# Quarter-array state products in a retention layer, and other issue times for a routed expert stage

## The chip, the cores and the metric

The kernel runs on one core of a Trainium2 chip. The metric is the device time of one execution in microseconds, the median of the runs. Five engines work side by side, each with its own instruction queue: TensorE (PE, matrix products; PEld is its loading of weights), VectorE (DVE), ScalarE (ACT), GpSimd (POOL) and SyncE (SP, which here only issues DMAs). They meet through semaphores.

## The reference

Three layers follow each other, all in fp32.

1. A retention layer: 8 sequences, 8 heads, 576 positions, head size 64. The scores are `q @ k.T / 8`, multiplied elementwise by `gamma_h ** (i - j)` for `j <= i` (0 elsewhere), and then multiplied by `v`. There is no softmax.
2. A first expert layer on the 4608 rows of 512: each row goes to the expert (of 8) with the largest cosine logit, `out = gate * (relu(x @ w1[e]) @ w2[e])` with 1024 hidden columns.
3. A second expert layer of 8 experts with a capacity of 576 rows each: all 4608 x 8 logits are sorted in falling order, and each is granted if its row is still free and its expert not yet full; then `relu(x @ w1[e]) @ w2[e]`.

```python
for idx in order:
    tok, e = (int(idx) // E, int(idx) % E)
    if assigned[tok] >= 0 or counts[e] >= cap:
        continue
    assigned[tok] = e
    counts[e] += 1
```

## The kernel before, in words

**Attention (lines 312 to 629).** The 4608 rows are 36 tiles of 128 rows; `T` counts them, `i = T % 9` is the place within a pair of sequences (nine tiles hold two sequences of 576 rows; in tile `i == 4` one sequence ends and the next begins). The eight heads are kept as four pairs `hp`, and a pair's two heads `e = 0, 1` stand in the two halves of the 128 partitions. The retention matrix is computed chunk by chunk: within a tile the scores `k.T q` are formed (`s_qk`, L401), weighted with the decay table (L404) and multiplied by `v` (`s_pv`, L419); what earlier tiles of the sequence contribute comes through a state per head of 64 x 64, which `s_state` accumulates in PSUM (L437) and copies to SBUF (L443). The state product is L415. Before the change the copy of the state is a block-diagonal 128 x 128 matrix per head pair (`bd`, two buffers whose other blocks are set to zero once), so that one product handles both heads with the whole array. The result `o` of a tile takes one PSUM bank, and ACT copies it out as `xT` (L422).

`s_out` (one tile later) computes routing logits from `xT` (L457, on four groups of 32 columns of the array) and transposes it back to rows (L463, into the PSUM tile `tp`, two buffers), which ACT copies out (L464). `s_sel` (two tiles later) finishes the logits (L472). Groups of up to five tiles are then routed (`route`): ranks by a product, destination rows by DVE, and scatters of the rows to DRAM on POOL's queue (L533). The order in which one loop step issues these parts is written out by hand at lines 592 to 622: loads of tile `T + 3` on SP's queue, `s_qk(T+1)`, `s_sel(T-2)`, `s_pv(T)`, a piece of routing, `s_state(T)`, `s_kd(T+2)`, `s_out(T-1)`. From tile 31 on the first expert weights are loaded and split into a high and a low part (`w_conv`: ACT L266, POOL L271).

A product of fp32 operands is two instructions in the trace, each with its own weight load, so 8 products are 16 instructions.

**First expert layer (lines 1221 to 1345).** Experts one after the other, three products per tile pair (high x high, high x low, low x high), rows loaded from the scattered copy in DRAM.

**Second expert layer (lines 1369 to 1536).** For each expert `p`: `search(p)` finds by bisection which logits are granted to it, in seven rounds, each of which goes through PE three times (counts L875, a fold L888, a decision L950) and through DVE between them; `members(p)` turns the chosen rows into an index list (L1106), POOL gathers the rows (five indirect DMAs, L1380), PE transposes them (L1400) and ACT and DVE split them (L1408, L1410); then come the first layer (`ffn1`, L1456) and the second (`ffn2`, L1495, and L1489 and L1491 for the last, half tile). Searches of later experts run beside the layers of earlier ones.

Their order on each engine is set by a planner, the class `Issue`: it keeps a clock for PE, DVE, ACT and POOL, and lets threads (the searches, member lists, splits, evacuations) issue their next step when its time by these clocks has come; PE's own layer products move PE's clock on. Its numbers are guesses at durations, and they decide only the order of issue. Two of them matter here:

- the sixth field of a thread, `early`: a thread's step on PE that follows a step on another engine is due `HOP["P"] - early` = 0.25 - early after it. A negative value makes the planner leave more time before it puts that step into PE's order. `search` and `members` get 0.7 for expert 0, 0.0 for expert 1 and `LAZY` = -0.35 for the others.
- `XGAT[p][t]`: when the planner thinks that gathered tile `t` has landed, its issue on POOL plus 3.2. `xtr2` lets the transposes into PE's order from then on (and from when the tile two before it has been split).

Of the kernel before, what the change touches and what calls it, by code (L numbers as in the profile page):

```python
# [9 lines left out]
F32 = mybir.dt.float32  # L10
# [3 lines left out]
AF = mybir.ActivationFunctionType  # L14
# [5 lines left out]
B, H, S, D = 8, 8, 576, 64  # L20
N, DM, E, FF = 4608, 512, 8, 1024
NT = N // 128
# [18 lines left out]

def constants():
    g = 1.0 - 2.0 ** (-5.0 - np.arange(H, dtype=np.float64))
    p = np.arange(128)
# [4 lines left out]
    for e in range(2):  # L49
        for hp in range(4):  # L50
            gq[64 * e:64 * e + 64, hp, :] = (g[2 * hp + e] ** s / 8.0)[None]
            gs[64 * e:64 * e + 64, hp, :] = (g[2 * hp + e] ** np.array([128.0, 256.0, 384.0]))[None]
# [11 lines left out]
    for nj in (32, 4, 2):  # L64
# [11 lines left out]
        "c_dt": np.ascontiguousarray(dt.reshape(128, 4, 2, 128).transpose(0, 2, 1, 3)).astype(f), "c_gq": gq.astype(f), "c_gs": gs.astype(f),  # L76
# [81 lines left out]
def moe_kernel(ctx: ExitStack, tc: tile.TileContext, moe_expert_emb, moe_tau, moe_w1, moe_w2,  # L158
# [153 lines left out]
    with tc.tile_pool(name="actab", bufs=1) as tab, \  # L312
# [20 lines left out]
        bd = []  # L333
        for i in range(2):
            t = tab.tile([128, 4, 128], F32, name=f"bd{i}")
            (G if i else V).memset(t, 0.0)
            bd.append(t)
# [69 lines left out]
        def s_pv(T):  # L407
            i = T % 9
            nq = nq_of(i)
            vt, sm = TL[T]["vr"], SM.pop(T)  # L410
            op_ = ps.tile([128, 4, 128], F32, name="o")
            if nq:
                qs, bdl = QS.pop(T), BD.pop(T)
                for hp in range(4):
                    P.matmul(op_[:, hp, :nq], bdl[:, hp, :], qs[:, hp, :nq], start=(hp == 0), stop=False,  # L415
                             skip_group_check=True)
            for hp in range(4):
                for e in range(2):
                    P.matmul(op_[64 * e:64 * e + 64, hp, :], vt[:, 2 * hp + e, :], sm[:, e, hp, :],  # L419
                             start=(hp == 0 and not nq), stop=True, skip_group_check=True)  # L420
            xT = wk.tile([128, 4, 128], F32, name="xT")
            A.activation(xT, op_, AF.Copy)  # L422
            XTT[T] = xT

        def s_state(T):
            i = T % 9
            t = TL.pop(T)
            if i == 8:
                return
            vt = t["vr"]  # L430
            r0 = 64 if i == 4 else 0
            kd = KDT.pop(T)
            if i in (0, 4):
                st_ps[0] = ps.tile([128, 4, 128], F32, name="st")
            for hp in range(4):
                for e in range(2):
                    P.matmul(st_ps[0][64 * e:64 * e + 64, hp, 64 * e:64 * e + 64], kd[r0:, 2 * hp + e, :],  # L437
                             vt[r0:, 2 * hp + e, :], start=(i in (0, 4) and hp == 0), stop=(i in (3, 7)),
                             skip_group_check=True)
            nb = bd[i % 2]  # L440
            for e in range(2):
                z = slice(64 * e, 64 * e + 64)
                A.activation(nb[z, :, z], st_ps[0][z, :, z], AF.Copy)  # L443
            BD[T + 1] = nb

        def s_out(T):
# [14 lines left out]
            xp = ps.tile([128, 4, 128], F32, name="tp", bufs=2)  # L461
# [409 lines left out]
    def search(p):  # L871
# [152 lines left out]
        IS.spawn(members(p, rk), p if p < 2 else 3, IS.t["V"], (0.7, 0.0, LAZY)[min(p, 2)])  # L1024
# [18 lines left out]
    NQ, LAZY = 4, -0.35  # L1043
# [17 lines left out]
    def members(p, rk):  # L1061
# [48 lines left out]
        XGAT[p] = [IS.t["G"] - 1.25 * (T2 - 1 - t) + 3.2 for t in range(T2)]  # L1110
# [4 lines left out]
    def chain():  # L1115
        for p in range(E):
            yield lambda: 0.0
            CHT[0][1] = (0, 3, 2)[min(p, 2)]
            CHT[0][5] = (0.7, 0.0, LAZY)[min(p, 2)]
            yield from search(p)  # L1120
# [454 lines left out]
```

## Time and profile before

| | |
|---|---|
| median of three timed runs | 1272.17 us (1271.94 to 1278.58) |
| profiled execution: its own time | 1273.87 us |
| profiled execution: span, mean granted clock | 1272.1 us, 0.969 |
| PE busy, share of the span | 1197.8 us, 94% |
| DVE, ACT, POOL busy | 716.4, 578.7, 326.3 us |
| attention, first to last score-value product | about 13 to 195 us |
| second expert layer, from its first product | about 746 to 1265 us |

The shares are averages over stages with different limits, so a stage is read from its own windows and its own order of time. PE's busy time is modelled from overlapping instructions; in its order of time the distances from one group's start to the next group's start are what work costs. The granted clock is 1.00 at 2.4 GHz and 0.50 at 1.2 GHz.

### The profile page before, as it was taken

The page shows a single profiled execution, that of the slowest core. Times are in us where ns is not written, and L with a number is a line of the kernel's source. Part 1 is how long each engine was busy: PE and PEld are TensorE (multiplying, and loading weights), DVE is VectorE, ACT ScalarE, POOL GpSimd, SP SyncE. Part 2 cuts the span into 40 slices and gives each one's busy share as a digit, 9 for nine tenths or more (in the row PEclk, how much of TensorE's full clock was granted, in tenths as well). Part 3 has the DMA queues.
Part 4 walks back from the last instruction along what each step waited for, and adds up shares of the span by engine and source line. Part 5 has one row for each costly group of instructions (what it writes and reads, how often), then busy time and mean ns, then how long its engine had stood idle before and what let it go on. Part 6 is the DMA issues. An engine that isn't in the chain of part 4 may idle for free. (4 is left out here: it accounts for less than half of the span.)

```text
span 1272.1 us, 23381 instructions
## 1 busy us (share of the span) xinstructions
PE 1197.8 (94%) x8855; PEld 1026.9 (81%) x8855; DVE 716.4 (56%) x2332; ACT 578.7 (45%) x1090; POOL 326.3 (26%) x451
## 2 busy tenths in 40 slices
PE   6999985899999999999999969998989899999997
PEld 5888874889898989899887667785968688788896
DVE  4466643767566757566666755656565657562120
ACT  3566653345454545453632152534434444455450
POOL 3253454613030313030100020404131313243211
PEclk9999986999999999999999979998989999999999
DMA  8898863576776868685851252938484737578841
GB/s 270 271 284 281 274 229 125 211 175 180 191 196 171 209 163 217 155 231 137 229 130 35 99 152 65 257 75 245 98 230 81 222 98 193 139 188 217 211 92 38
DMA packets 91741, 224.63 MB, mean 177 GB/s; under 512 B 13671, under 2 KB 14447, under 8 KB 91488
## 3 DMA queue, kind: packets, MB, share of 16 engines
q0 software_dynamic: 28272, 90.35, 32.6%
q1 hardware_dynamic: 63344, 132.67, 31.3%
q8 instruction: 72, 1.18, 0.4%
q14 instruction: 53, 0.43, 0.1%
HBM read 130.26 MB, written 40.28 MB: 134 GB/s over the span
## 5 line engine op out<-in xcount | busy, mean ns | idle before, releaser
L1167 DVE SCALAR_TENSOR_TENSOR jk<-yr,wgb 128x512 bf16<-128x512 f32 x168 | 115.4, 687 | 2.4
L1246 ACT ACTIVATE hh<-l 128x320 fp32r<-128x320 f32 x128 | 55.4, 433 | 120.1 <-PE l L1245 106.2
L1438 DVE SCALAR_TENSOR_TENSOR h2l<-l,h2h 128x288 fp32r<-128x288 f32 (+2 forms) x128 | 58.3, 457 | 79.0 <-ACT h2h L1436 78.6
L1247 DVE SCALAR_TENSOR_TENSOR hl<-l,hh 128x320 fp32r<-128x320 f32 x128 | 62.4, 487 | 66.4 <-ACT hh L1246 60.9
L251 POOL DMA_DIRECT2D w_0l<-raw x29 | 26.2, 903 | 285.8 <-ACT w_0l L248 247.2
L1333 ACT ACTIVATE yr<-l,gts 128x512 f32<-128x512 f32 x40 | 27.5, 688 | 152.1 <-PE l L1321 70.8
L1436 ACT ACTIVATE h2h<-l 128x288 fp32r<-128x288 f32 (+2 forms) x128 | 52.3, 409 | 90.5 <-PE l L1456 89.8
L1470 POOL DMA_INDIRECT out_dram<-o,tid x40 | 41.0, 1025 | 162.8 <-ACT o L1463 122.4
L404 DVE TENSOR_TENSOR sm<-s,dt 128x512 f32<-128x512 f32 (+1 forms) x80 | 48.0, 633 | 55.3 <-PE s L401 43.8
L1463 ACT ACTIVATE o<-l 128x512 f32<-128x512 f32 (+1 forms) x40 | 23.8, 595 | 111.2 <-PE l L1495 79.5
L1380 POOL DMA_INDIRECT xg<-ybuf,idx x40 | 43.0, 1075 | 75.4 <-SPq L1348 53.4
L717 DVE TENSOR_TENSOR xl<-tp,xh 128x512 fp32r<-128x512 f32 (+1 forms) x41 | 27.6, 676 | 53.1 <-ACT xh L716 53.1
L401 PE MATMUL s<-qT,kT 64*128 64x128 f32 x576 | 45.0, 297 | 11.2 <-DMA qT<-qT 9.1
L931 DVE TENSOR_TENSOR cmp<-v,kb 128x1280 bf16<-128x1280 f32 (+1 forms) x42 | 54.4, 1295 | 0.2
L401 PEld LDWEIGHTS s<-qT,kT 64*128 64x128 f32 x576 | 37.7, 198 | 17.4 <-DVE nw_u L168 4.9
L1243 PE MATMUL l<-xh,w_0h 128*128 128x320 f32 x128 | 40.9, 319 | 10.3 <-DVE hl L1247 5.7
L378 POOL TENSOR_TENSOR kd<-kr,gk 128x512 f32<-128x512 f32 (+1 forms) x32 | 34.5, 1080 | 59.8 <-PE st L437 23.9
L251 POOL DMA_DIRECT2D w_3l<-raw x29 | 24.8, 854 | 94.1 <-ACT w_3l L248 70.6
L533 POOL DMA_INDIRECT xs<-xg,r_sli x36 | 36.9, 1024 | 46.8 <-ACT xg L464 26.3
L1408 ACT ACTIVATE xh<-tp 128x512 fp32r<-128x512 f32 (+1 forms) x40 | 22.0, 552 | 58.6 <-PE tp L1400 44.2
L422 ACT ACTIVATE xT<-o 128x512 f32<-128x512 f32 x36 | 21.5, 597 | 59.0 <-PE o L419 51.6
L251 POOL DMA_DIRECT2D w_2l<-raw x29 | 25.2, 868 | 88.9 <-ACT w_2l L248 64.1
(374 smaller groups left out, 4084.0 us busy)
## 6 DMA issues: line engine op xcount, KB each, us to landing
raw<-in_moe_w_dram SPq DMA_DIRECT2D x128, 512.0 KB
w_0l<-raw POOLq DMA_DIRECT2D x29, 512.0 KB
w_1l<-raw POOLq DMA_DIRECT2D x29, 512.0 KB
w_2l<-raw POOLq DMA_DIRECT2D x29, 512.0 KB
w_3l<-raw POOLq DMA_DIRECT2D x29, 512.0 KB
ybuf<-yr SPq DMA_DIRECT2D x40, 257.0 KB
xt<-xs SPq DMA_DIRECT2D x39, 261.0 KB
kT<-kT SPq DMA_DIRECT2D x36, 256.0 KB
```

The costliest lines, as they stand in the source:

```text
L251: G.dma_start(lo, RAW[wpos[1]], accum_op=OP.add)
L401: P.matmul(sp[e][:, hp, :], kT[r, hp, :], qT[r, hp, :], start=True, stop=True, skip_group_check=True)
L404: V.tensor_tensor(sm[z, e, :, z], sp[e][z, :, z], dt_t[z, e, :, z], op=OP.mult)
L931: V.tensor_tensor(cmp, bc(v, ALLC, nj), kb.bitcast(F32)[:, None, :].to_broadcast([128, NSL, nj]), op=OP.is_ge)
L1167: V.scalar_tensor_tensor(jk, yr[:, :DM], 1.0, wgb[:, j, :], op0=OP.mult, op1=OP.mult, accum_out=L2V[:, cc, j:j + 1])
L1243: P.matmul(pp, wh[:, fz], xh[:, kk, z], start=(kk == 0), stop=False)
L1246: A.activation(hh[:, f, z], pp, AF.Relu)
L1247: V.scalar_tensor_tensor(hl[:, f, z], pp, 0.0, hh.bitcast(F32)[:, f, z], op0=OP.max, op1=OP.subtract)
L1380: G.indirect_dma_start(out=xg[:m, t, :], out_offset=None, in_=ybuf, in_offset=bass.IndirectOffsetOnAxis(ap=idx[:m, t:t + 1], axis=0))
L1436: A.activation(h2h[:, f, z], pq, AF.Relu)
L1438: V.scalar_tensor_tensor(h2l[:, f, z], pq, 0.0, h2h.bitcast(F32)[:, f, z], op0=OP.max, op1=OP.subtract)
L1470: st = G.indirect_dma_start(out=out, out_offset=bass.IndirectOffsetOnAxis(ap=TID[p][:m, t:t + 1], axis=0), in_=o[:m], in_offset=None)
```

## The change

It has three parts.

1. The state is kept dense, 128 x 64 per head pair, with one copy per tile instead of two. Each state product becomes two products, each on a quarter of the array (64 rows by 64 columns). So that four products that follow each other name the four quarters, the two heads of every odd pair change places in the partitions (`head`), in the tables and in the laid-out inputs `kT` and `qT`; the results go back to the places they had. Pairs of even and odd number write to two PSUM banks, so `o` takes two banks, and the transposes' tile `tp` has one buffer instead of two. The score-value product L419 names the array's column halves in the order low, high, high, low.
2. In the second expert layer the planner's landing time of gathered rows is 4.8 instead of 3.2 for all experts but the first.
3. `LAZY` has a value for each expert.

```diff
--- before.py
+++ after.py
@@ -39,6 +39,10 @@
 LOG2E = 1.4426950408889634
 
 
+def head(e, hp):
+    return 2 * hp + (e ^ (hp & 1))
+
+
 def constants():
     g = 1.0 - 2.0 ** (-5.0 - np.arange(H, dtype=np.float64))
     p = np.arange(128)
@@ -48,8 +52,8 @@
     gq, gs = np.empty((128, 4, 128)), np.empty((128, 4, 3))
     for e in range(2):
         for hp in range(4):
-            gq[64 * e:64 * e + 64, hp, :] = (g[2 * hp + e] ** s / 8.0)[None]
-            gs[64 * e:64 * e + 64, hp, :] = (g[2 * hp + e] ** np.array([128.0, 256.0, 384.0]))[None]
+            gq[64 * e:64 * e + 64, hp, :] = (g[head(e, hp)] ** s / 8.0)[None]
+            gs[64 * e:64 * e + 64, hp, :] = (g[head(e, hp)] ** np.array([128.0, 256.0, 384.0]))[None]
     tl = np.arange(9)[None, :, None]
     pos = 128 * tl + p[:, None, None]
     pos = np.where(pos >= S, pos - S, pos)
@@ -73,7 +77,7 @@
     s16[np.arange(16), np.arange(16) % E] = 1.0
     return {
         **blk, "c_s16": s16,
-        "c_dt": np.ascontiguousarray(dt.reshape(128, 4, 2, 128).transpose(0, 2, 1, 3)).astype(f), "c_gq": gq.astype(f), "c_gs": gs.astype(f),
+        "c_dt": np.stack([np.stack([dt[:, head(e, hp)] for hp in range(4)], 1) for e in range(2)], 1).astype(f), "c_gq": gq.astype(f), "c_gs": gs.astype(f),
         "c_gk": gk.reshape(128, 72).astype(f), "c_sel": sel.astype(f),
         "c_id": np.eye(128, dtype=f), "c_tri": tri.astype(f),
     }
@@ -330,11 +334,7 @@
         dt_t = tab.tile([128, 2, 4, 128], F32, name="dt")
         SY.dma_start(dt_t, c["c_dt"])
         load_tile(0, ("vr", "kr"))
-        bd = []
-        for i in range(2):
-            t = tab.tile([128, 4, 128], F32, name=f"bd{i}")
-            (G if i else V).memset(t, 0.0)
-            bd.append(t)
+        bd = [tab.tile([128, 4, 64], F32, name=f"bd{i}") for i in range(2)]
         taub = tab.tile([128, 1], F32, name="taub")
         SY.dma_start(taub, ap(moe_tau, 0, [[0, 128], [1, 1]]))
         emb = tab.tile([E, DM], F32, name="emb")
@@ -408,18 +408,25 @@
             i = T % 9
             nq = nq_of(i)
             vt, sm = TL[T]["vr"], SM.pop(T)
-            op_ = ps.tile([128, 4, 128], F32, name="o")
+            op_ = ps.tile([128, 2, 512], F32, name="o")
+
+            def o(e, hp, n):
+                c0 = 64 * (e ^ (hp & 1))
+                return op_[c0:c0 + 64, hp & 1, 128 * (hp >> 1):128 * (hp >> 1) + n]
             if nq:
                 qs, bdl = QS.pop(T), BD.pop(T)
                 for hp in range(4):
-                    P.matmul(op_[:, hp, :nq], bdl[:, hp, :], qs[:, hp, :nq], start=(hp == 0), stop=False,
-                             skip_group_check=True)
+                    for e in range(2):
+                        r = slice(64 * e, 64 * e + 64)
+                        P.matmul(o(e, hp, nq), bdl[r, hp, :], qs[r, hp, :nq], start=(hp < 2), stop=False,
+                                 skip_group_check=True)
             for hp in range(4):
                 for e in range(2):
-                    P.matmul(op_[64 * e:64 * e + 64, hp, :], vt[:, 2 * hp + e, :], sm[:, e, hp, :],
-                             start=(hp == 0 and not nq), stop=True, skip_group_check=True)
+                    P.matmul(o(e, hp, 128), vt[:, head(e, hp), :], sm[:, e, hp, :],
+                             start=(hp < 2 and not nq), stop=True, skip_group_check=True)
             xT = wk.tile([128, 4, 128], F32, name="xT")
-            A.activation(xT, op_, AF.Copy)
+            A.activation(xT.rearrange("p (j s) n -> p s j n", s=2),
+                         op_[:, :, :256].rearrange("p s (j n) -> p s j n", j=2), AF.Copy)
             XTT[T] = xT
 
         def s_state(T):
@@ -431,16 +438,14 @@
             r0 = 64 if i == 4 else 0
             kd = KDT.pop(T)
             if i in (0, 4):
-                st_ps[0] = ps.tile([128, 4, 128], F32, name="st")
+                st_ps[0] = ps.tile([128, 4, 128], F32, name="st")[:, :, :64]
             for hp in range(4):
                 for e in range(2):
-                    P.matmul(st_ps[0][64 * e:64 * e + 64, hp, 64 * e:64 * e + 64], kd[r0:, 2 * hp + e, :],
-                             vt[r0:, 2 * hp + e, :], start=(i in (0, 4) and hp == 0), stop=(i in (3, 7)),
+                    P.matmul(st_ps[0][64 * e:64 * e + 64, hp, :], kd[r0:, head(e, hp), :],
+                             vt[r0:, head(e, hp), :], start=(i in (0, 4) and hp == 0), stop=(i in (3, 7)),
                              skip_group_check=True)
             nb = bd[i % 2]
-            for e in range(2):
-                z = slice(64 * e, 64 * e + 64)
-                A.activation(nb[z, :, z], st_ps[0][z, :, z], AF.Copy)
+            A.activation(nb, st_ps[0], AF.Copy)
             BD[T + 1] = nb
 
         def s_out(T):
@@ -458,7 +463,7 @@
                          skip_group_check=True)
             part = wk.tile([128, 128], F32, name="part")
             A.activation(part, lp[:, :128], AF.Copy)
-            xp = ps.tile([128, 4, 128], F32, name="tp", bufs=2)
+            xp = ps.tile([128, 4, 128], F32, name="tp")
             for hp in range(4):
                 P.transpose(xp[:, hp, :], xT[:, hp, :], ident)
             A.activation(xg[:, i, :DM], xp.rearrange("p a n -> p (a n)"), AF.Copy)
@@ -1021,7 +1026,7 @@
             V.scalar_tensor_tensor(sn[:, z], sn[:, z], r2[:, z:z + 1], mem[:, z], op0=OP.add, op1=OP.mult)
         V.scalar_tensor_tensor(rk, sn[:, 0], 1000.0, sn[:, 1], op0=OP.add, op1=OP.add)
         LST.append(p)
-        IS.spawn(members(p, rk), p if p < 2 else 3, IS.t["V"], (0.7, 0.0, LAZY)[min(p, 2)])
+        IS.spawn(members(p, rk), p if p < 2 else 3, IS.t["V"], LAZY[p])
         if p < E - 1:
             yield "V", 1.2
             fo = tl("fo", (128, E))
@@ -1040,7 +1045,7 @@
 
     LST, MDONE, CHT = [], {}, []
     shf = sw.tile([128, 256], BF, name="shf")
-    NQ, LAZY = 4, -0.35
+    NQ, LAZY = 4, (0.7, 0.0, 0.0, -0.2, -0.35, -0.5, -0.5, -0.5)
 
     RROK = {}
 
@@ -1107,7 +1112,7 @@
         MDONE[p] = IS.t["V"]
         yield lambda: GATHER[0](p)
         yield "G", 1.25 * T2
-        XGAT[p] = [IS.t["G"] - 1.25 * (T2 - 1 - t) + 3.2 for t in range(T2)]
+        XGAT[p] = [IS.t["G"] - 1.25 * (T2 - 1 - t) + (4.8 if p else 3.2) for t in range(T2)]
         XG2[p] = GATHER[1](idx)
 
     GATHER = [lambda p: None, None]
@@ -1116,7 +1121,7 @@
         for p in range(E):
             yield lambda: 0.0
             CHT[0][1] = (0, 3, 2)[min(p, 2)]
-            CHT[0][5] = (0.7, 0.0, LAZY)[min(p, 2)]
+            CHT[0][5] = LAZY[p]
             yield from search(p)
 
     with tc.tile_pool(name="mb", bufs=1, reuse_waits="tile") as mb, tc.tile_pool(name="mw", bufs=2, reuse_waits="tile") as mw, \
@@ -1559,7 +1564,8 @@
     q, k, v = (np.asarray(inputs[n]) for n in ("q", "k", "v"))
     laid = {nm: np.ascontiguousarray(a.transpose(0, 2, 1, 3)).reshape(N, DM) for nm, a in (("kr", k), ("vr", v))}
     for nm, a in (("kT", k), ("qT", q)):
-        t = a.transpose(1, 3, 0, 2).reshape(4, 2, D, NT, 128)
+        t = a.transpose(1, 3, 0, 2).reshape(4, 2, D, NT, 128).copy()
+        t[1::2] = t[1::2, ::-1].copy()
         laid[nm] = np.ascontiguousarray(t.transpose(3, 1, 2, 0, 4)).reshape(NT, 128, 4, 128)
     laid["w_gate_t"] = np.ascontiguousarray(np.asarray(inputs["moe2_w_gate"]).T)
     for name, a in laid.items():
```

## Rows read from the trace of the kernel before

**Rows 1.** Windows by stage: engines' busy time, granted clock, DMA share, GB/s.
```profile
20.00:160.00 140.00, 139.22 (x1983) 118.32 (x1982) 84.72 (x215) 85.24 (x225) 53.39 (x74) 0.99 0.85 280
160.00:212.00 52.00, 34.94 (x405) 28.56 (x404) 21.57 (x91) 24.37 (x59) 26.34 (x34) 0.81 0.47 167
...
735.00:1272.00 537.00, 507.19 (x3394) 422.27 (x3394) 263.01 (x813) 236.13 (x448) 139.18 (x180) 0.95 0.60 153
```

**Rows 2.** PE's timeline, one tile of attention: start, us, line, tiles, instructions.
```profile
114.42 0.42 PE L457 MATMUL lg<-xT,enT 128*32 128x128 f32 x8
114.78 0.66 PE L463 MATMUL tp<-ident,xT 128*128 128x128 f32 x4
...
116.46 0.39 PE L472 MATMUL lg<-sel,part 128*128 128x8 f32 x2
116.70 1.14 PE L415 MATMUL o<-qs,bd 128*128 128x128 f32 x8
117.77 1.09 PE L419 MATMUL o<-sm,vr 128*64 128x128 f32 x16
118.69 0.64 PE L437 MATMUL st<-vr,kd 128*64 128x64 f32 x16
119.26 0.43 PE L457 MATMUL lg<-xT,enT 128*32 128x128 f32 x8
```

**Rows 3.** The same view, a tile that has no state product.
```profile
102.64 0.39 PE L472 MATMUL lg<-sel,part 128*128 128x8 f32 x2
102.96 1.09 PE L419 MATMUL o<-sm,vr 128*64 128x128 f32 x16
```

**Rows 4.** All instructions of the state product's line on PE.
```profile
L415 PE MATMUL o<-qs,bd x256: 275/275/580, 20.1 to 193.2; 128*128 128x128 f32 x112, 128*128 128x64 f32 x16
```

**Rows 5.** Windows of 20 us in attention, the one with the highest DMA share.
```profile
60.00:80.00 20.00, 19.50 (x284) 16.76 (x285) 14.41 (x34) 12.28 (x35) 10.86 (x15) 1.00 0.94 296
```

**Rows 6.** ACT's timeline, the copy of the transposed tile.
```profile
116.25 0.59 ACT L464 ACTIVATE xg<-tp 128x512 f32<-128x512 f32 x1
```

**Rows 7.** Timelines of POOL, ACT and PE around tile 32; in brackets the idling before.
```profile
165.07 1.04 POOL L378 TENSOR_TENSOR kd<-kr,gk 64x512 f32<-64x512 f32 x1 [5.03 <-DMA xs<-xg,r_sli]
...
176.63 1.06 ACT L266 ACTIVATE w_0h<-raw 128x1024 fp32r<-128x1024 f32 x1 [6.53 <-DMA raw<-in_moe_w_dram]
...
179.34 0.59 PE L472 MATMUL lg<-sel,part 128*128 128x8 f32 x2 [4.65 <-ACT part L460]
```

**Rows 8.** Line L875, counts of searches 1 and 2 (ten instructions each).
```profile
L875 PE MATMUL srb<-oh,cmp x60: 176/176/190, 752.6 to 781.1; 128*128 128x32 bf16 x50, 128*16 128x32 bf16 x10
...
L875 PE MATMUL srb<-oh,cmp x70: 176/176/190, 804.4 to 846.0; 128*128 128x32 bf16 x60, 128*16 128x32 bf16 x10
```

**Rows 9.** PE's timeline at the turns from one expert to the next.
```profile
815.69 0.46 PE L1400 MATMUL tp<-ident,xg 64*128 64x64 f32 x4
...
880.01 0.66 PE L1400 MATMUL tp<-ident,xg 128*128 128x128 f32 x4 [1.56 <-DMA xg<-ybuf,idx]
...
890.04 0.61 PE L1456 MATMUL l<-xh,w_0h 128*128 128x288 f32 x1
...
945.01 0.63 PE L1400 MATMUL tp<-ident,xg 128*128 128x128 f32 x4 [1.72 <-DMA xg<-ybuf,idx]
946.93 1.09 PE L1400 MATMUL tp<-ident,xg 128*128 128x128 f32 x4 [1.29 <-DMA xg<-ybuf,idx]
...
1016.99 0.66 PE L1400 MATMUL tp<-ident,xg 128*128 128x128 f32 x4 [2.16 <-DMA xg<-ybuf,idx]
```

**Rows 10.** POOL's timeline, the second gather of expert 3.
```profile
938.71 1.01 POOL L1380 DMA_INDIRECT xg<-ybuf,idx  x1 [0.30 <-issue]
```

**Rows 11.** Windows with the clock at its lower level, columns as in rows 1.
```profile
881.80:895.40 13.60, 11.74 (x55) 9.09 (x56) 8.39 (x20) 4.36 (x11) 0.91 (x1) 0.50 0.28 85
946.60:953.50 6.90, 6.57 (x19) 4.69 (x20) 3.25 (x7) 1.18 (x3) 1.06 (x2) 0.51 0.47 164
1018.30:1021.70 3.40, 3.40 (x20) 2.71 (x19) 1.19 (x4) 0.52 (x2) 0.00 (x0) 0.50 0.54 187
```

## The prediction

> **What bounds the kernel now.** I read the windows by stage first, then TensorE's own order of time in both stages that the diff touches, then what its late instructions waited for. Each row of [rows 1] gives a stretch, its length, the busy time and instruction count of PE, PEld, DVE, ACT and POOL, the granted clock, the DMA share and GB/s. From 20 to 160 us, tiles of attention, PE is busy 139.22 of 140 us: whatever shortens PE's work there shortens the stage. From 160 to 212 us it is busy 34.94 of 52: there a chain through weights and scatters rules. From 735 us on, the second expert stage, PE is busy 507.19 of 537 at a granted clock of 0.95: what can be won without removing PE work is some 30 us of idling and what the 0.50 level costs.
>
> **Part 1, dense states.** A tile's period is 119.26 - 114.42 = 4.84 us [rows 2]. Between the start of the selection product (L472) and the start of the score-value product (L419) lie 1.31 us, which hold the four state products of L415, each two instructions: 8 on the whole array. The change makes them 16 on quarters of it.
>
> No row has quarter products, so I bound them. In tiles without a state L419 starts 0.32 us after L472 [rows 3]: that is what the change of array shape costs, and the change now pays it ahead of its own first product, then the change of shape into L419, as before. The nearest row with four at once is L457: its 8 instructions on four column groups take 0.36 us to the next group, two rounds of four, draining included. L419's 16, in eight rounds of two, take 118.69 - 117.77 = 0.92, so 0.115 a round. With four at once, L415 needs four rounds: 0.36 + 2 x 0.115 = 0.59, and L472 to L419 becomes 0.32 + 0.59 = 0.91: **0.40 us less a tile**. With two at once it is eight rounds: 0.36 + 6 x 0.115 + 0.32 = 1.37, 0.06 more than now. One after the other it is sixteen: 2.29, 0.98 more. I take four at once: the halves overlap by columns in L419, and by columns four at a time in L457, and consecutive products of the change name four different quarters.
>
> There are 256 / 8 = 32 such tiles [rows 4]; the four of 64 columns I count like the others. Not all of it arrives. At tile 32 PE waits 4.65 us at 179.34 for an activation that stands behind the first weight conversion, which starts at 176.63 when its weights land; SP issues them behind a load that waits for scatters, and POOL at 165.07 waits for those same scatters' landing [rows 7]. That chain is released about tile 29 and then runs at its own pace, so what tiles 29 to 31 save only lengthens the wait: 29 tiles count, 29 x 0.40 = 11.6, less 0.6 for the first tiles, where PE waits for loads: **-11 us**.
>
> What hides the rest. The copy of the state, one 128x256 activation for two of 64x256, leaves ACT less to do; ACT is 85 of 140 us busy [rows 1], so nothing, and at most some tenths at the tail. The copy xT reads two banks, the same 512 columns: between 0 and 0.1 us a tile, hidden for the same reason. The transposes' PSUM tile is now single: the copy out of it starts at 116.25 and takes 0.59 [rows 6], and the next transposes come at about 119.6, 2.4 us of cover even at the shorter period; without that cover each tile would lose what is missing of 0.59. L419 now alternates its column halves as low, high, high, low. Pairs remain, so zero; if the places where one half follows itself (three a tile) cost a round each, 3 x 0.115 x 36 = 12 us. I take zero, since pairs are what L419 needs. The removed memsets stand beside the first loads: nothing.
>
> Loads must keep up. A tile moves about 1.3 MB; the densest stretch, 60 to 80 us, shows 296 GB/s at a share of 0.94 [rows 5], and 280 GB/s on the mean of 20 to 160. At 4.44 us a tile the mean becomes 280 x 4.84 / 4.44 = 305. Free capacity is nearly gone, but loads run three tiles ahead; zero, with 4 us as the other end.
>
> **Part 2, the second stage's order.** Here nothing is added or removed; the planner's numbers decide where in PE's order the search's products and the transposes of gathered rows stand. For search 2 the slack before each PE step goes from 0.35 to 0, for search 3 from 0.35 to 0.2, for searches 5 to 7 from 0.35 to 0.5. Search 1 already has 0: its six counts run from 752.6 to 781.1, 5.7 us a round; search 2's seven from 804.4 to 846.0, 6.9 a round [rows 8]. With three PE steps a round, 3 x 0.35 = 1.05 is the planned difference. Seven rounds and four further steps make 8.8; I take **8 us earlier for the index list of expert 2**.
>
> What that buys stands at the turn from expert 1 to 2: the transposes at 880.01 wait 1.56 us for gathered rows, little of the second layer is left to run by then, and expert 2's first layer starts at 890.04 [rows 9]. From 881.8 to 895.4 the clock is 0.50 (the 1.2 GHz level, after the idling) and PE is busy 11.74 of 13.6 us [rows 11]: lost are 1.56 + 1.9 idle and half of 11.74, 9.3 us together. Eight us earlier, second-layer products still cover most of the landing. What stays is the landing itself: the second gather of expert 3 ends its issue at 938.71 + 1.01, and its transposes run at 946.93, 7.2 us later [rows 9, 10]; the planner allowed 3.2, now 4.8, so some 2 us of waiting plus a short fall of the clock stay: gain 2 to 9.3, I take 6.
>
> At the turns 2 to 3 and 3 to 4 there is product work left, so 1.6 us more allowance turns 1.6 us of waiting (1.72 + 1.29 at 945 to 947; 2.16 at 1017) into products [rows 9], and may save the falls of the clock, worth half of 6.57 and of 3.40 busy us [rows 11]. Gains 1.6 to 4.9 and 1.6 to 3.3; I take 2.5 and 2. At the turn 0 to 1 the last transposes at 815.69 stand just before the end of the second layer's products and no wait is seen [rows 9]: pushed back by 1.6 they are exposed, with their split behind them. Cost 0 to 4, I take 2. Queued behind them is all of expert 1's first layer. Later turns show no such wait; searches 5 to 7 get slower by 7 x 3 x 0.15 = 3 us each, against an 8 us head start: zero. Sum: -6 - 2.5 - 2 + 2 = **-8.5 us**.
>
> **Total.** The profiled execution took 1273.87 us, its span 1272.1 and 1.8 around it; the three timed runs' median, 1272.17, lies 1.7 below. 1273.87 - 11 - 8.5 = 1254.4 on that execution, 1252.7 on the median: **1253**.
>
> **Rivals.**
> 1. *Two quarters at a time* (0.12). The first two products of each four use different row halves and write one PSUM bank. L401, the one product here with two row halves, writes two banks, so no row shows such a pair running together. If bank sharing forbids it, rounds hold two, L472 to L419 takes 1.37, and attention gains nothing (2 us lost): 1272.2 + 2 - 8.5 = 1265.7. The Trainium skill, TensorEngine Tiling (Array Packing), Restrictions and Gotchas, says that different row tiles cannot access the same PSUM bank simultaneously; by that rule this rival is the outcome, and no run shown so far tests it.
> 2. *The reordering gives nothing* (0.14). The landing is 7.2 us, not 4.8, so every turn still waits and the clock still falls, and the turn 0 to 1 pays 4: only attention's 11 remain: 1261. For it: the allowance is still 2.4 short. Against it: 8 us of search time are read from two searches side by side.
> 3. *Loads bind* (0.07). At 305 GB/s the queue falls behind and 4 to 6 us of attention's gain go to waits of L401 for qT or kT: 1258.
> 4. *Slower* (0.05). Quarter products run one at a time. Place: L415, 32 tiles; price 0.98 each, 31 us, none of it absorbed; it decides from more than eight rounds a tile on. 1272.2 + 31 - 8.5 = 1295. Against it: L419's halves overlap.
>
> The forecast itself has 0.62, its own range 1245 to 1261. The range to hold the time 8 in 10 reaches to rivals 2 and 3 and most of 1: 1243 to 1265. What a measurement of this kernel tells from no change is about 0.5%, 6.4 us: faster than 1265.8 takes 0.61 of the forecast and 0.24 of rivals 1 to 3, 0.85; within it 0.09 (halves of rivals 1 and 2); slower 0.06.
>
> **What would show it.** Right: L415 as 512 instructions of 64*64; L419 starting 0.9 us after L472; a period near 4.44; the wait at tile 32 a microsecond longer; search 2's rounds under 6 us; no long 0.50 stretch at the turn 1 to 2, and transposes of expert 3 waiting 1.4 us or less. Wrong: 1.3 us or more between L472 and L419, waits of L401 for loads in mid-stage, or transposes that wait as long as before although they stand later; a longer pause at the turn 0 to 1 than 4 us would eat the second part.

## The result and the profile after

The changed kernel takes 1253.04 us (median of four runs, 1251.50 to 1253.45) against 1273.45 for the kernel before beside it; the ratio is 0.983, 95% interval 0.980 to 0.986. Run once more on another chip (below) it took 1247.84 against 1274.44, ratio 0.980, interval 0.977 to 0.982. The forecast was 1253. That the number fits so well is partly luck, as the stages show: two terms were off and a third, unforeseen one made up for it.

The profiled execution took 1252.89 us, its span is 1251.1, which is 21.0 less than before. Cut at the first product of each expert layer, the span up to its last product divides like this (us; 7.2 us follow the last product in both kernels):

| | before | after | forecast | measured |
|---|---|---|---|---|
| attention, to the first product of expert layer 1 | 212.3 | 202.4 | -11 | -9.9 |
| expert layer 1, to the first product of the second | 534.1 | 538.8 | 0 | +4.7 |
| second stage: expert 0 (turn 0 to 1 in it) | 70.2 | 72.0 | +2 | +1.8 |
| experts 1, 2, 3 together | 217.2 | 199.0 | -10.5 | -18.2 |
| experts 4 to 7 together | 231.1 | 231.7 | 0 | +0.6 |

**Attention.** The windows of the changed kernel, with the columns of [rows 1]; the line numbers are larger by five to seven than before from L415 on.

```profile
20.00:160.00 140.00, 136.41 (x2299) 112.05 (x2301) 85.68 (x228) 80.67 (x209) 54.64 (x77) 0.99 0.87 291
...
725.00:1251.00 526.00, 498.69 (x3404) 418.65 (x3404) 266.54 (x818) 237.95 (x451) 140.84 (x180) 0.97 0.62 157
60.00:80.00 20.00, 19.95 (x345) 16.41 (x347) 15.65 (x41) 12.02 (x32) 9.21 (x15) 1.00 0.92 295
```

PE is nearly as full as before from 20 to 160 us (136.41 of 140 us, where it was 139.22), in 316 more instructions. The loads still keep up: 291 GB/s on the mean. PE's order of time in one tile, which answers to [rows 2], and the list of all instructions of the state product, which answers to [rows 4]:

```profile
107.58 0.42 PE L462 MATMUL lg<-xT,enT 128*32 128x128 f32 x8
...
109.62 0.39 PE L477 MATMUL lg<-sel,part 128*128 128x8 f32 x2
109.93 0.67 PE L421 MATMUL o<-qs,bd 64*64 64x128 f32 x16
110.53 1.09 PE L425 MATMUL o<-sm,vr 128*64 128x128 f32 x16
111.46 0.64 PE L444 MATMUL st<-vr,kd 128*64 128x64 f32 x16
112.02 0.43 PE L462 MATMUL lg<-xT,enT 128*32 128x128 f32 x8
```
```profile
L421 PE MATMUL o<-qs,bd x512: 218/269/356, 19.0 to 182.4; 64*64 64x128 f32 x149, 64*64 64x64 f32 x22
```

The tile's period is 112.02 - 107.58 = 4.44 us, where it was 4.84. L477 to L425 is 110.53 - 109.62 = 0.91 us, where it was 1.31. The next line starts 0.60 us after the 16 instructions of the quarter products began (0.59 forecast). That they are four rounds of four can be read from the single instructions in the trace: they start in groups of four, each group within 0.02 us, at 109.93, 110.09, 110.20 and 110.31. L425 to L444 is 0.93, as before, so the order low, high, high, low of its column halves costs nothing. The end of the stage, in brackets the idling before (answers to [rows 7]): first the line of the kernel before that takes `kd`, without a wait; then PE and POOL of the changed kernel.

```profile
166.38 0.68 PE L437 MATMUL st<-vr,kd 64*64 64x64 f32 x16
```
```profile
159.05 0.83 PE L444 MATMUL st<-vr,kd 64*64 64x64 f32 x16 [2.18 <-POOL kd L378]
166.35 0.42 PE L462 MATMUL lg<-xT,enT 128*32 128x128 f32 x8 [0.52 <-DVE slot L525]
171.12 0.39 PE L477 MATMUL lg<-sel,part 128*128 128x8 f32 x2 [2.66 <-ACT part L465]
175.48 1.16 PE L401 MATMUL s<-qT,kT 64*128 64x128 f32 x16 [0.95 <-DMA qT<-qT]
181.27 0.66 PE L468 MATMUL tp<-ident,xT 128*128 128x128 f32 x4 [0.92 <-ACT xg L469]
```
```profile
157.84 1.17 POOL L378 TENSOR_TENSOR kd<-kr,gk 64x512 f32<-64x512 f32 x1 [6.55 <-DMA xs<-xg,r_sli]
```

The POOL instruction that stands behind the scatters is released at 157.84 instead of 165.07, 7.2 us earlier, while PE is ready for its result at 159.05 - 2.18 = 156.87 instead of 166.38, 9.5 earlier. So PE now waits for `kd` where it had not to before, and the wait for the first weights has shrunk from 4.65 to 2.66. The last row is the single `tp` buffer: it costs 0.92 us once.

**Second stage.** The transposes of gathered rows at the turns 1 to 2, 2 to 3 and 3 to 4, and the first layer of expert 2 (answers to [rows 9]); none has a wait in brackets any more (before there were six such waits, 8.3 us together; [rows 9] has four of them, and the other two are shown here first):

```profile
881.79 1.09 PE L1400 MATMUL tp<-ident,xg 128*128 128x128 f32 x4 [1.13 <-DMA xg<-ybuf,idx]
...
1018.09 0.94 PE L1400 MATMUL tp<-ident,xg 128*128 128x128 f32 x4 [0.45 <-DMA xg<-ybuf,idx]
```

```profile
870.19 1.04 PE L1405 MATMUL tp<-ident,xg 128*128 128x128 f32 x8
...
882.57 0.30 PE L1461 MATMUL l<-xh,w_0h 128*128 128x288 f32 x1
...
928.42 1.03 PE L1405 MATMUL tp<-ident,xg 128*128 128x128 f32 x8
...
991.58 1.03 PE L1405 MATMUL tp<-ident,xg 128*128 128x128 f32 x8
```

And the windows over these turns (columns as above): the clock is 1.00 throughout, where [rows 11] had 23.9 us at 0.50. The first line is a new stretch at 0.50, which stands behind the turn 0 to 1, after two waits of PE for search steps (1.12 and 0.40 us).

```profile
814.80:818.20 3.40, 3.40 (x16) 3.40 (x15) 1.92 (x3) 1.57 (x3) 0.00 (x0) 0.50 0.49 166
868.00:950.00 82.00, 80.53 (x576) 64.32 (x575) 50.73 (x159) 35.09 (x70) 22.50 (x32) 1.00 0.61 161
950.00:1020.00 70.00, 69.69 (x506) 57.76 (x505) 40.55 (x134) 34.70 (x65) 21.57 (x25) 1.00 0.64 160
```

All of the gain in experts 1 to 3 is waiting and clock: in their 217.2 us before, PE stood idle for 13.0 and lost 10.9 to the lower clock (half of its busy time at 0.50), in the 199.0 after it is 3.7 and 1.7. What remains is 193.4 and 193.5.

**Where the transfers stand.** SP and POOL up to expert 3's gather, first of the kernel before, then of the changed one. The SP row covers several weight loads of 512 KB (x3, x2); `xg` is a gather, `w_2l` and `w_3l` are the 512 KB transfers that finish a weight block.

```profile
933.46 10.05 SPq L239 DMA_DIRECT2D raw<-in_moe_w_dram  x3
932.36 0.85 POOL L251 DMA_DIRECT2D w_2l<-raw  x1 [3.68 <-PE srb L950]
...
934.88 0.87 POOL L251 DMA_DIRECT2D w_3l<-raw  x1 [0.33 <-issue]
937.35 1.06 POOL L1380 DMA_INDIRECT xg<-ybuf,idx  x1 [1.60 <-DVE idx L1106]
```
```profile
920.09 3.47 SPq L243 DMA_DIRECT2D raw<-in_moe_w_dram  x2
920.90 1.07 POOL L1385 DMA_INDIRECT xg<-ybuf,idx  x1 [2.54 <-PE srb L955]
922.28 1.42 POOL L1385 DMA_INDIRECT xg<-ybuf,idx  x1 [0.30 <-issue]
...
927.42 1.01 POOL L255 DMA_DIRECT2D w_2l<-raw  x1
...
929.77 0.92 POOL L255 DMA_DIRECT2D w_3l<-raw  x1
```

Before, the gather of expert 3 came behind the transfers of `w_2l` and `w_3l` and amid three loads; now it comes ahead of `w_2l` and `w_3l`, with two loads beside it. Measured from the start of the expert whose products run, it is earlier by 937.35 - 890.04 - (920.90 - 882.57) = 9.0 us.

### The profile page after: what moved, and what is told of

The parts are those of the page before. It is cut to its first block, busy times and chain, and to the rows that moved or that the text cites. A ratio compares the mean times of both kernels' runs of the same rounds, so it can differ in the third digit from the quotient of the medians.

```text
span 1251.1 us, 23851 instructions
## 1 busy us (share of the span) xinstructions
PE 1181.0 (94%) x9111; PEld 1012.0 (81%) x9111; DVE 715.4 (57%) x2331; ACT 567.6 (45%) x1058; POOL 326.5 (26%) x450
## 5 line engine op out<-in xcount | busy, mean ns | idle before, releaser
L401 PE MATMUL s<-qT,kT 64*128 64x128 f32 x576 | 44.8, 296 | 11.5 <-DMA qT<-qT 9.7
L401 PEld LDWEIGHTS s<-qT,kT 64*128 64x128 f32 x576 | 37.6, 198 | 17.9 <-issue 5.7
L255 POOL DMA_DIRECT2D w_1l<-raw x29 | 25.1, 867 | 88.9 <-ACT w_1l L252 61.8
```

What stands on the lines that cost most here:

```text
L255: G.dma_start(lo, RAW[wpos[1]], accum_op=OP.add)
L401: P.matmul(sp[e][:, hp, :], kT[r, hp, :], qT[r, hp, :], start=True, stop=True, skip_group_check=True)
```

## The experiments

All were timed in five rounds beside the kernel before. In the texts, expert n of the second stage lasts from its first product to that of the next.

**One part at a time.** `e1_dense` has the dense states and the planner's old numbers, `e2_planner` the old attention and the new numbers.

```diff
 e1_dense, against the changed kernel
-    NQ, LAZY = 4, (0.7, 0.0, 0.0, -0.2, -0.35, -0.5, -0.5, -0.5)
+    NQ, LAZY = 4, (0.7, 0.0, -0.35, -0.35, -0.35, -0.35, -0.35, -0.35)
-        ... + (4.8 if p else 3.2) for t in range(T2)]
+        ... + 3.2 for t in range(T2)]
```

> The dense states and quarter products alone; the planner's landing time and slack are those of before. Theory (the parts add, and quarter products are worth 0.40 us a tile): the first product of the first expert layer 9.9 us earlier than before, L477 to L425 0.91 us, about 1263 us, and up to 1268 if the clock falls again behind the two idle spells of the first expert layer (3.1 us before its second layer's weights, 1.9 us before its last expert), which both kernels have and after which it fell only in the changed one. Rival (the first expert layer gives the gain back for good, because its loads keep their own pace): no more than 5 us faster than before, 1268, in every run. Rival of chance (clock falls decide): the first expert layer's length, 522.3 us after and 517.6 before, goes either way here.

> Attention as before; landing time 4.8 and the graded slack alone. Theory of the prediction: 8.5 us faster, 1264.5. Theory from the trace of the changed kernel (second stage 15.8 us shorter): 1257, with experts 1, 2 and 3 at about 69, 66 and 63 us from first layer to first layer. Rival (the second stage was shorter because attention ended earlier, not by its own order): under 3 us faster, 1270.

`e1_dense`: 1262.61 us (about 1263 expected), ratio 0.992 (0.989 to 0.995); experts 1 to 3 217.3, as before. `e2_planner`: 1254.70 (1257 expected from the changed kernel's trace), ratio 0.985 (0.982 to 0.988); experts 1 to 3 198.9, second stage 504.1. So the planner's numbers are worth about twice the dense states. The two alone add up to some 25 us (8.7 and 16.6 against 1271.32 beside them).

**Landing and slack apart.** `e3_land32` is the changed kernel with the landing time 3.2, `e4_oldslack` with the slack 0.35 from expert 2 on.

```diff
 e3_land32
-        ... + (4.8 if p else 3.2) for t in range(T2)]
+        ... + 3.2 for t in range(T2)]
 e4_oldslack
-    NQ, LAZY = 4, (0.7, 0.0, 0.0, -0.2, -0.35, -0.5, -0.5, -0.5)
+    NQ, LAZY = 4, (0.7, 0.0, -0.35, -0.35, -0.35, -0.35, -0.35, -0.35)
```

> The changed kernel with the landing time back at 3.2 for all experts, slack graded. Theory (landing time is worth 1.6 us of waiting and a fall of the clock at each of the turns 1 to 2, 2 to 3 and 3 to 4, and costs 2 at the turn 0 to 1): transposes wait 1.5 to 3 us for gathered rows at those three turns, 1256 to 1260. Rival (slack alone made the turns, the earlier index lists leave time enough): no such waits, and the turn 0 to 1 is 2 us shorter: 1251.

> The changed kernel with slack 0.35 for all experts from 2 on, landing time 4.8. Theory (slack is worth 8 us of search time for expert 2, of which the turn 1 to 2 keeps 4 to 6, and some of the turns after it): index list of expert 2 some 8 us later, waiting and the lower clock back at the turn 1 to 2, 1259 to 1262. Rival (landing time alone does it): 1253, the same as the changed kernel.

`e3_land32`: 1250.97, ratio 0.983 (0.979 to 0.986), second stage 505.7. `e4_oldslack`: 1250.60, ratio 0.982 (0.979 to 0.985), second stage 506.3. Both theories are off by 5 us and more (1256 to 1260 and 1259 to 1262), and the rivals' times (1251 and 1253) are nearer, although some waits came back.

Against 518.1 to 518.5 without either edit, each alone takes 12 to 13 us off the second stage. Both together take 12 to 16 off (502.6 to 506.6 in the five profiles with both, mean 504.1), and the ratios of the three kernels' timed runs cannot be told apart (0.983, 0.982, and 0.983 and 0.980 for the changed kernel). They do not add: my separate prices for them were the wrong picture. The clock shows where they overlap: half of PE's busy time at 0.50 in the second stage is 14.9 and 15.4 us without either edit, 7.9 with either one, and 6.3 to 11.3 with both. What the stage takes without that part is 503.0 and 503.2 with neither, 497.8 and 498.3 with one, 494.6 to 496.3 with both. So one edit alone already saves about as much of the clock's cost as both do, and the second saves some 1.5 to 4 us of other time.

What each leaves is seen in PE's order of time, first of `e3_land32`, then of `e4_oldslack`:

```profile
924.28 0.66 PE L1405 MATMUL tp<-ident,xg 128*128 128x128 f32 x4 [1.81 <-DMA xg<-ybuf,idx]
```
```profile
868.12 0.74 PE L1405 MATMUL tp<-ident,xg 128*128 128x128 f32 x4 [1.44 <-DMA xg<-ybuf,idx]
...
934.12 1.39 PE L1405 MATMUL tp<-ident,xg 128*128 128x128 f32 x8 [1.29 <-DMA xg<-ybuf,idx]
```

**Two quarters instead of four.** `e5_twoq` leaves the heads in their places, so the state products name two quarters only.

```diff
-    return 2 * hp + (e ^ (hp & 1))
+    return 2 * hp + e
...
-                c0 = 64 * (e ^ (hp & 1))
+                c0 = 64 * e
...
-        t[1::2] = t[1::2, ::-1].copy()
```

> The changed kernel with the heads left in their places: the state's quarter products then name only two quarters of the array (rows and columns low, rows and columns high), the same 16 instructions a tile. Theory (rounds: what shortens the state products is that four different quarters follow each other): two at a time, eight rounds, L477 to L425 takes 1.37 us instead of 0.91, 0.46 x 29 tiles = 13 us more, period 4.90: 1264 to 1267. Rival A (the four run one behind the other at the rate at which instructions come, and which quarter they name does not matter): L477 to L425 0.9 to 1.0, time 1251 to 1255. Rival B (two row halves into one bank never run together): one at a time, 2.29, 40 us more: about 1293.

1257.44, ratio 0.985 (0.982 to 0.988). A tile of it in PE's order of time:

```profile
111.19 0.39 PE L477 MATMUL lg<-sel,part 128*128 128x8 f32 x2
111.51 1.09 PE L421 MATMUL o<-qs,bd 64*64 64x128 f32 x16
112.53 1.09 PE L425 MATMUL o<-sm,vr 128*64 128x128 f32 x16
```

L477 to L425 is 1.34 (1.37 expected for eight rounds), the single instructions start in pairs, and attention ends at 211.5, 11 us later than the mean of the kernels with four quarters (200.3). Its time lies 9 to 11 us above those of the next two runs, made on the same chip with four quarters (1246.74 and 1248.58; their planner's numbers differ a little, see below); 13 were expected. Rivals A and B fall: which quarters follow each other decides, so the exchange of heads is what makes the dense states pay.

**The first turn, and the late searches.** `e6_land_p2` applies 4.8 only from expert 2 on; `e7_slack23` leaves searches 5 to 7 at 0.35.

```diff
 e6_land_p2
-        ... + (4.8 if p else 3.2) for t in range(T2)]
+        ... + (4.8 if p > 1 else 3.2) for t in range(T2)]
 e7_slack23
-    NQ, LAZY = 4, (0.7, 0.0, 0.0, -0.2, -0.35, -0.5, -0.5, -0.5)
+    NQ, LAZY = 4, (0.7, 0.0, 0.0, -0.2, -0.35, -0.35, -0.35, -0.35)
```

> The changed kernel with the landing time 3.2 for experts 0 and 1, and 4.8 from expert 2 on. Theory (at the turn 0 to 1 nothing waited, so the longer allowance only exposes the last transposes there): expert 0 takes 70 to 70.6 instead of 72.0, experts 1 to 3 stay within 1 us of 69.4, 66.2, 63.4: 1.5 us less, 1249 to 1252. Rival (searches run beside expert 0, so an earlier turn only moves the wait for the index list of expert 2): expert 0 70.2, expert 1 71: same time as the changed kernel, 1252 to 1254.

> The changed kernel with the slack of searches 5 to 7 left at 0.35 (0 and 0.2 for searches 2 and 3 as changed). Theory (later turns have their rows long before they are needed, so the 0.5 does nothing): experts 0 to 3 identical to the changed kernel, experts 4 to 7 66.6, 59.6, 53.9, 51.6 within 1 us each, sum within 2: 1251 to 1255. Rival (the larger slack keeps PE from standing at a search step too early): waits at search steps in experts 2 to 4 return, 3 us or more slower: 1256 or more.

`e6_land_p2`: 1246.74 (1249 to 1252 expected), ratio 0.976 (0.973 to 0.979); expert 0 71.0 (70 to 70.6 expected) and expert 1 67.9 instead of 72.0 and 69.4, second stage 499.8, 2.8 less than the changed kernel's, so nothing of the first turn's gain is given back. The 1.5 us in expert 1 were not expected: the stretch at 0.50 behind the turn 0 to 1 is gone. `e7_slack23`: 1248.58, ratio 0.978 (0.975 to 0.981); second stage 501.7. Its experts 3 and 4 moved by +2.6 and -3.1, more than the 1 us expected, but the sum is the same: the 0.5 for searches 5 to 7 earns nothing.

**What makes the rows late.** `e8_light` is the kernel before, order unchanged, without 56 of the weight loads.

```diff
+            if wpos[0] >= 8 * E + 8:
+                raw = RAW[8 * E + 7]
+            else:
+                raw = stg.tile([128, FF], F32, name="raw")
-            raw = stg.tile([128, FF], F32, name="raw")
+            if wpos[0] >= 8 * E + 8:
+                pass
-            if two:
+            elif two:
```

> The kernel before, with the weight loads of experts 1 to 7 of the second stage left out (their high and low parts are made of a block that stays in SBUF, so the results of these experts are not the reference's); the order on PE, ACT, DVE and POOL is unchanged, 56 transfers of 512 KB on SP's queue are gone. Theory L (the rows of a gather land late because weight loads stand in the DMA engines among them): from the end of the second gather's issue to its transposes 5 us or less at the turns 1 to 2, 2 to 3 and 3 to 4 instead of 6.9, 7.2, 6.7; the waits there (1.56, 1.72 + 1.29, 2.16) under 0.5 each, and with them the half-clock stretches of 13.7, 6.8 and 3.4 us at these turns: experts 1 to 3 together 10 to 19 us shorter, 1253 to 1263. Rival G (the gather's own row descriptors set the landing): the three landings within 0.7 us of before, the waits over 1 us each, time 1268 to 1274.

1258.06, ratio 0.986 (0.983 to 0.989). PE's waits from 800 to 1035 us in the three kernels (total, times, longest); first before, then changed, then `e8_light`:

```profile
PE tp L1400 <- DMA xg<-ybuf,idx: 8.3, 6, 2.2
PE srb L875 <- DVE cmp L931: 3.2, 4, 1.2
...
```
```profile
PE srb L955 <- DVE fl L952: 1.8, 2, 1.4
PE srb L893 <- DVE cs L889: 1.4, 2, 1.1
PE srb L880 <- DVE cmp L936: 1.3, 1, 1.3
...
```
```profile
PE srb L880 <- DVE cmp L936: 4.0, 5, 1.2
PE tp L1405 <- issue: 1.2, 1, 1.2
...
```

No transpose of `e8_light` waits for its rows. From the end of the second gather's issue to its transposes pass 3.9, 3.9 and 3.7 us at the three turns, where it was 6.9, 7.2 and 6.7, and experts 1 to 3 take 202.3 instead of 217.2. The gather's own rows and their number are the same; the weight loads among them made them late.

The trace's DMA packets say it without PE: a gather's packets (4112 bytes, two rows each, 288 for the five gathers of an expert) can be told from the others by their size. Here is the time (us) from the end of the first gather's issue to the first such packet, and from the end of the fifth's issue to the end of the last:

| | turn 1 to 2 | turn 2 to 3 | turn 3 to 4 |
|---|---|---|---|
| before | 4.4, 4.4 | 3.6, 5.1 | 3.1, 4.5 |
| changed | 3.6, 4.3 | 2.0, 3.3 | 2.0, 4.0 |
| changed, repeated (`e9_after`) | 2.3, 5.7 | 2.0, 3.1 | 2.0, 4.2 |
| `e3_land32` | 2.4, 3.6 | 4.1, 5.0 | 0.7, 2.0 |
| `e8_light` | 1.2, 1.9 | 1.6, 2.0 | 0.7, 1.7 |

Without the loads both times are shorter at every turn. With them, the changed order shortens both only at the turn 2 to 3; at the others the first rows come earlier and the last ones hardly.

**The changed kernel again, its better version, and the same removal from it.** `e9_after` repeats it, `e10_both` joins the edits of `e6_land_p2` and `e7_slack23`, and `e11_light` makes the edit of `e8_light` in the changed kernel.

> The changed kernel itself once more, on the chip of the next two runs, so that they can be compared with it: ratio to the kernel before 0.978 to 0.985; second stage (first product to end) 502 to 504 us; expert layer 1 (first product to the second stage's first) 534 to 540, as chance has it.

> The changed kernel with landing 3.2 for experts 0 and 1, and the slack of searches 5 to 7 back at 0.35. Theory (each of the two alone was worth 1 to 3 us of the second stage in the runs so far): second stage 498 to 500 us, 3 us less than the changed kernel beside it, ratio to the kernel before 0.975 to 0.980. Rival (what one turn gains the next gives back, as with slack and landing): second stage 501 to 503, time within 1 us of the changed kernel.

> The changed kernel with the weight loads of experts 1 to 7 of the second stage left out (the results of these experts are not the reference's). Theory (the changed order no longer waits for the gathered rows, so late landing costs it nothing any more): second stage 500 to 503 us, within 2 of the changed kernel, although the same removal took 12 us from the second stage of the kernel before. Rival (the loads cost in more ways than by late rows): 6 us or more shorter here too, 497 or less.

`e9_after`: ratio 0.980 (0.977 to 0.982), attention to 199.6, expert layer 1 536.8, second stage 502.6, the same as in the first profile. `e10_both`: 1247.22, ratio 0.981 (0.978 to 0.983; 0.975 to 0.980 expected); its second stage is shorter, 499.7, but its time beside `e9_after` (1247.84) is no different that could be measured. `e11_light`: 1248.29, ratio 0.980 (0.978 to 0.982), second stage 504.5: the removal that took 16 us from the second stage of the kernel before (518.5 to 502.1; the 12 in my expectation were wrong) takes nothing from the changed one (a little over the 500 to 503 expected). Late rows are a cost that the changed order hardly has any more.

## Why the prediction was right, and where it was not

**Attention: right mechanism and size.** Four quarters ran at once, 0.40 us a tile, to the hundredth. Rival 1 is excluded here: of each four quarters that run together two have different row halves and write one bank. The Trainium skill, TensorEngine Tiling (Array Packing), Restrictions and Gotchas, says that different row tiles cannot access the same PSUM bank simultaneously; this trace does not agree, for products whose results go to different partitions of the bank: the 16 take 0.60 us and start four at a time, where two at a time, in `e5_twoq`, take 1.02. One reading was loose: the 0.32 us of [rows 3] are not the cost of a change of array shape but the whole distance from L472 to the next line. Without a change of shape that distance is 116.70 - 116.46 = 0.24 [rows 2], so the change itself costs about 0.08. The sum used distances alone and is not hurt.

**The end of attention: the wrong wait.** I let the saved time of tiles 29 to 31 lengthen the wait at tile 32 by a microsecond. It became 2 us shorter, and the loss appeared at 159.05 for `kd`, behind the scatters. PE's waits of 0.2 us and more from 145 us to the end of the tiles are 5.2 us before (0.52 + 4.65) and 7.5 after (0.23 + 2.18 + 0.52 + 2.66 + 0.95 + 0.92): 2.3 of the tiles' gain. Over all profiles attention ends at 198.2 to 202.6 with dense states in four quarters (nine profiles, mean 200.3) and at 206.4 to 212.3 without (three, mean 210.1): 9.8 us.

**Second stage: right in sign, too small; the step that failed is "what stays is the landing itself".** I took 7.2 us from the issue of a gather to its rows as a constant, so that some 2 us of waiting and a fall of the clock had to stay at the turn 1 to 2, and at the turns 2 to 3 and 3 to 4 only 1.6 us could be won by the longer allowance. It is not a constant. From the end of the second gather's issue to its transposes pass at most 3.9 us without weight loads (`e8_light`), and 5.1, 5.2 and 5.4 in the changed kernel, where no transpose had to wait (in its repetition one waited 0.37 us, at 5.7). At the turn 2 to 3 the gather now stands ahead of weight transfers that it stood behind. But an earlier index list does not do that by itself: `e3_land32`, `e6_land_p2` and `e10_both` have the changed kernel's slack for search 3, and there the gather stands behind `w_2l` and amid three loads again, its second rows are ready only after 6.6, 6.9 and 6.7 us, and waits of up to 1.81, 0.88 and 0.69 us are back (`e3_land32` has a row in the table of packets, 4.1 and 5.0). Where a gather falls among the loads was forecast by no step.

The step ahead of it was mis-sized too, the other way. Search 2's rounds are 5.9 us instead of 6.9, as forecast, but its index list comes 63.0 us after its first count instead of 67.6: 4.6 us earlier, not 8. I had also let this head start end at its own turn, but it was handed on: the gathers are issued 6.4, 9.0 and 9.8 us earlier within their expert at the three turns.

What stood to be won at the three turns, by the prediction's own reading of the waits and of half the busy time at 0.50, was 9.3 + (1.72 + 1.29 + 3.3) + (2.16 + 1.7) = 19.5 us; with the two waits that it did not have (1.13 and 0.45) it is 21. 18.2 were won, 10.5 forecast. Experts 1, 2 and 3 are shorter by 4.1, 7.6 and 6.5. Of the clock's cost, 2.7 us of the turn 1 to 2 lay in expert 2, and 1.7 of the new stretch behind the turn 0 to 1 lie in expert 1 now; so the three turns gave about 8.6, 4.9 and 6.5 (6, 2.5 and 2 forecast). The turn 0 to 1 costs 1.8 in expert 0, which looks like the 2 forecast, and with that stretch 3.5. Its later transposes are of the longer allowance: with 3.2 there, expert 0 takes 71.0 and 69.4 (`e6_land_p2`, `e10_both`), and the stretch is gone in both.

**Expert layer 1: +4.7 us that no step had.** PE's waits within the layer are nearly the same in both kernels, but what the clock did after them is not. First the kernel before, around its idling at 245 us and at 665 us, then the changed kernel, then `e2_planner`:

```profile
248.21 0.41 PE L1243 MATMUL l<-xh,w_0h 128*128 128x320 f32 x1 [3.16 <-DVE hl L1247]
...
245.10:251.90 6.80, 3.69 (x25) 3.69 (x26) 6.53 (x18) 0.86 (x2) 5.96 (x10) 1.00 0.59 183
665.40:668.80 3.40, 1.53 (x11) 1.53 (x11) 3.30 (x10) 0.44 (x1) 0.00 (x0) 1.00 0.32 60
```
```profile
238.74 0.63 PE L1248 MATMUL l<-xh,w_0h 128*128 128x320 f32 x1 [3.13 <-DVE hl L1252]
...
238.00:244.80 6.80, 6.06 (x23) 6.07 (x24) 6.49 (x32) 0.44 (x1) 5.70 (x11) 0.50 0.46 136
661.20:664.60 3.40, 3.40 (x15) 2.86 (x14) 3.21 (x14) 0.95 (x2) 0.00 (x0) 0.50 0.00 0
```
```profile
240.30:247.10 6.80, 5.83 (x22) 5.83 (x23) 6.49 (x30) 0.44 (x1) 5.73 (x11) 0.50 0.45 141
```

Half of 6.06 + 3.40 busy us at 0.50 is 4.7, the whole difference. (The wait at 665 us is 1.87 in both.) It is not of the change: `e2_planner`, whose attention is the old one, falls at the same place, and so does `e8_light`, which is the kernel before up to the second stage. Over all profiles the layer takes 534.1, 536.9 and 540.0 with the old attention and 534.4 to 539.9 (ten, mean 537.3) with the dense states. The clock explains nearly all of it: half of PE's busy time at 0.50 within the layer goes from 5.5 us (before) to 12.1 (`e8_light`), and without it the layer takes 526.8 to 528.6 us in all thirteen. The profile of before was at the lucky end. Without this term the change is worth 9.8 us in attention and 12 to 16 in the second stage (mean 14.3), some 24 together, not the 19.5 of the forecast. The first comparison shows 1273.45 - 1253.04 = 20.4, the repeated one 1274.44 - 1247.84 = 26.6. So the forecast of 1253 was met in part by luck: in the profiled execution the second stage gave 15.8 us instead of 8.5, and the lower clock in a stage outside the change took 4.7 of that back. Why the clock falls after such a pause in one execution and not in the next stays open.

**Zeros.** The `tp` buffer (0.92 us once), the two-bank copy, the column order and the loads (291 GB/s on the mean, no wait of L401 for loads between the first two tiles and 175 us) cost what was said, next to nothing. Rival 2 (reordering gives nothing) fell with `e2_planner`, rivals 3 and 4 with the tile's period of 4.44 us.

## What to carry to other kernels

A landing time read while the DMA engines are full belongs to what else is queued at that moment, and not to the transfer; before such a number goes into a sum as a constant, look at what stands ahead of it on the other queues, and at where among those an earlier issue would fall. Two edits that remove the same wait are not to be priced one by one: each alone gave 12 to 13 us, both together 12 to 16. And where one execution stands on each side, compare the stages that the change does not touch first: here they hid 5 us of the gain.

## What the hardware showed unexpectedly

- The same pause of PE (3.13 to 3.16 us before one product of expert layer 1) stands in all thirteen profiles. It was followed by 6.8 us at 0.50 in eight of them, among these the changed kernel and `e2_planner`, by 3.4 us in four, among these the changed kernel's repetition, and by a clock of 1.00 in the kernel before.
- At nearly the same DMA share while the gathers ran (1.02 to 1.04 before, 0.97 to 1.04 after) the second gather's rows were ready in 6.7 to 7.2 us in one order and in 5.1 to 5.4 us or less in the other: here the share alone did not tell how long a transfer waits.
